# Gated linear attention and four experts on one core: earlier w2 splits, a tile of its own for the last raw w1, and other due times for the attention steps

## The chip, the core and the metric

The kernel runs on one core of a Trainium2 chip. The metric is the device time of one execution in microseconds. Each kernel is run several times and its median is taken; the kernel before has a median of 972.38 us over three runs (972.06 to 972.76). In what follows PE is TensorE (matmuls; PEld its weight loads), ACT is ScalarE, DVE is VectorE, POOL is GpSimd and SP is SyncE, which issues most of the loads.

## The reference

A gated linear attention over 4 batches, 8 heads, 768 tokens and a head width of 48 gives a matrix of 3072 tokens by 384, and four experts with a hidden width of 1024 work on each of its rows, weighted by each token's probabilities.

```python
# attention: q, k, v, alpha of shape (4, 8, 768, 48)
for t in range(S):
    state = alpha[:, :, t, :, None] * state + np.einsum('bhd,bhe->bhde', k[:, :, t], v[:, :, t])
    y[:, :, t] = np.einsum('bhd,bhde->bhe', q[:, :, t], state)
# bridge: (B,H,S,D) -> (B*S, H*D)
x = y.transpose(0, 2, 1, 3).reshape(B * S, H * D)
# experts: w1 (4, 384, 1024), w2 (4, 1024, 384)
p = domain_probs / (domain_probs.sum(-1, keepdims=True) + 1e-09)
for e in range(E):
    h = np.maximum(x @ w1[e], 0.0)
    out += p[:, e:e + 1] * (h @ w2[e])
```

## The kernel before

**Units and groups.** The tokens are cut into 24 units of 128 (six blocks of the sequence, four batches each; the block is the outer loop). Units are counted from 0 here. The attention of a unit (`attention`, for unit 0 `first_unit`) is a generator that does a step and yields: first the transposes of alpha, k and q, with the unit's own terms (`own_terms`, L524), then products of cumulated decays level by level (`next_q` L566, `next_k` L580, the ACT copies at L559 and L579), between them two bursts of small matmuls: the "products" (96 matmuls at L587) and the "far" burst (L663, L668 and L587). DVE takes pieces of their scores into a tile `near` (L597), ACT (L678, L681) and POOL (L686) copy these into `lat`, and then comes the result: matmuls of the state with the queries and of the values with `lat` (`yps`, L708), the copy out of PSUM (L721), the matmuls of the state's update (`sps`, L745) and that update (L753 on DVE in the first block; L755 on POOL and L756 on DVE later).

**Experts.** Units are gathered into seven groups: units 0 and 1, then groups of four, and a last one of two. For each group and expert, `up` multiplies by w1 (eight chunks of the hidden width, index `fc`; result `one`, relu into `hT`) and `down` by w2 (result `ops`, added to `acc` at L926). Group 0 computes in plain fp32 (L820, L905). From group 1 on, weights, inputs and hidden values are held as a rounded top and a remainder, and the product is three matmuls of fp32r parts (L826, L905); the remainder of the hidden values is taken at L851, that of x at L292.

**Weights.** Each expert's w1 and w2 come in four pieces. A raw piece is loaded by `load_piece` (SP, L255). `split_piece` makes its parts: for w2 a POOL cast of the whole (L263), an ACT pass for the top (L268), a DVE subtraction for the remainder (L270), and mostly a store to a kept copy in DRAM (POOL's queue, L276), from which later groups load it (L232, L236, with a short load on POOL's queue, L222). w1 is split while group 0 works, w2 while group 1 does. A split advances by one step with each call of `background`; `making` is the list of splits that have not begun. In the kernel before, the raw w1 of experts 1 to 3 is loaded, in turn, into parts of the tiles that later hold w2 (`shared`), at chunk 4 of the expert before; the raw w2 of the first expert of group 1 is loaded at the end of the last `up` of group 0. Two pieces of it are split in the last `down` of group 0 and two in the first `up` of group 1 (the second entry of `BESIDE`).

**Order.** The order of instructions is written out by hand: each engine does its instructions in the order in which the program issues them. `deal` gives each step of each unit a due time on a clock of estimated costs (`cost`), spread over the time from one group to the next by the shares in `BEATS`; `advance` is called beside every chunk of the experts' work and runs the steps that are due. Two rules in `deal` are touched here: a step waits for the step of the unit before that frees its buffer (`ahead`), and the products of a unit (step 8) are not put closer than 2.5 behind the result (step 16) of the one before. The steps of unit 1 up to its `lat` copies are put by a list of times in the main part; it is worked off, whatever is left of it, after the first `down`.

PSUM has four buffers for `one` and `ops` together, two for scores and two for `yps` and `sps`. SP's and POOL's queues are worked in order too: a load that waits for a buffer or for a store holds back what is issued behind it.

Of the kernel before, what the change touches and what calls it, by code (L numbers as in the profile page):

```python
# [10 lines left out]
F32 = mybir.dt.float32  # L11
F32R = mybir.dt.float32r
# [8 lines left out]
def kernel(  # L21
# [37 lines left out]
    nc = tc.nc  # L59

    B, H, S, D = q.shape
    E, DM, F = moe_w1.shape
    P = 128
# [5 lines left out]
    KC = DM // P  # L69
    FCH = F // P  # L70
    NT = B * P
    NQ = 4
    QF = F // NQ
# [9 lines left out]
    j = np.arange(P)[:, None] % HALF  # L83
# [10 lines left out]
    wts = ctx.enter_context(tc.tile_pool(name="wts", bufs=2))  # L94
# [14 lines left out]
    near = const.tile([P, H, QUAD], F32, name="near")  # L109
# [46 lines left out]
    casts = deque()  # L156
    beat = [0]
    shared = {}
    accs = {}


# [45 lines left out]


    SPLIT_AT = {1: 2, 4: 3}
    BESIDE = [{1: 0, 2: 1, 3: 2, 4: 3}, {1: 2, 2: 3}]  # L210

    def second(rest):
        return wts.tile([P, 1 if rest else 2, KC * QF], F32R, name="w2r" if rest else "w2", bufs=NQ)
# [10 lines left out]
    def load_piece(l, i, beside=False, rest=False):  # L224
        if i >= E * NQ * LAST:
            return
        gi, k = divmod(i, E * NQ)
        e, c = divmod(k, NQ)
        if gi > l and not (l == 1 and fresh(gi, e)):
            if l == 0:  # L230
                w = wt[l][i] = wts.tile([P, 3, KC * QF], F32R, name="w1", bufs=AHEAD)
                nc.sync.dma_start(out=w[:, :2].bitcast(F32), in_=kept[l][k])  # L232
                casts.append((beat[0], lambda: load_short(l, i, w[:, 2])))
                return
            w = second(rest)
            nc.sync.dma_start(out=w[:, :1].bitcast(F32), in_=kept[l][k][:, 1:] if rest else kept[l][k][:, :1])  # L236
            if not rest:
                casts.append((beat[0], lambda: load_short(l, i, w[:, 1])))
            wt[l].setdefault(i, []).append(w)
            return  # L240
        if l == 1 and gi == 0 and not beside:
            return
        if l == 0:

            if e == 0:
                shared[c] = second(True)[:, 0], second(False)[:, 1]
            w = shared[c][e % 2].bitcast(F32)
        elif gi > 0 or e == 1:
            if c == 0:
                shared["w2"] = hid.tile([P, NQ, KC * QF], F32, name="raw2", bufs=1)  # L250
            w = shared["w2"][:, c]
        else:
            w = hidden[c][:, 0].rearrange("p f n -> p (f n)")[:, :KC * QF].bitcast(F32)
        wt[l][i] = w
        nc.sync.dma_start(out=w.rearrange("p (c n) -> p c n", c=(KC, FPQ)[l]), in_=whole_piece(l, i))  # L255

    def split_piece(l, i):
        gi, k = divmod(i, E * NQ)
        whole = wt[l][i]
        if i >= E * NQ:  # L260
            ws = wt[l][i] = [second(False), second(True)]
            top, rest = (w[:, 0] for w in ws)
            nc.gpsimd.tensor_copy(out=ws[0][:, 1], in_=whole)  # L263
        else:
            ws = [wts.tile([P, 3, KC * QF], F32R, name="w1", bufs=AHEAD)]
            top, rest = (ws[0][:, part] for part in range(2))

        nc.scalar.activation(out=top, in_=whole, func=ACT.Copy, scale=LIFT)  # L268
        yield
        nc.vector.tensor_sub(rest, whole, top.bitcast(F32))  # L270
        if (gi, k // NQ) != (1, 0):
            yield
            to = kept[l][k]
            for part, w in enumerate(ws):
                n = 2 - l
                nc.gpsimd.dma_start(out=to[:, part:part + n], in_=w[:, :n].bitcast(F32))  # L276
# [219 lines left out]
    def attention(u):  # L496
# [186 lines left out]
        yield  # L683
        for s in range(P // QUAD):
            rows = slice(QUAD * s, QUAD * (s + 1))
            nc.gpsimd.tensor_copy(out=lat[rows, :, rows], in_=near[rows])  # L686
        KT = KTs[-1]
        yield

# [4 lines left out]
        def result():  # L694
# [16 lines left out]
            if slot == 0:  # L711
# [5 lines left out]
                    xraws[gi] = xraws[gi].rearrange("p (c n) -> p c n", n=NT)  # L717
                else:
                    xraws[gi] = []
            if gi < LAST:  # L720
                nc.scalar.copy(out=xraws[gi][:, :, slot * P:(slot + 1) * P], in_=yps)  # L721
            else:

                xraws[gi].append(AT)
                nc.scalar.copy(out=AT[:, :KC, :], in_=yps)
# [62 lines left out]
    def up(gi, e, fc, slots=None):  # L788
# [13 lines left out]
            making.append(split_piece(1, first_piece(gi, e) + beside[fc]))  # L802
        if gi == 0 and e > 0 and fc in SPLIT_AT:
            making.append(split_piece(0, e * NQ + SPLIT_AT[fc]))
        if gi == 0 and e + 1 < E and fc == FCH // 2 and begins:
            for k in range(NQ):
                load_piece(0, (e + 1) * NQ + k)
            for k in range(NQ if e == 0 else 0):
                load_piece(1, NQ + k, beside=True)
# [24 lines left out]
        background()  # L834
        if f == FPQ - 1 and ends:
            if gi == 0:
                for k in range(NQ if i == E * NQ - 1 else 0):
                    load_piece(1, i + 1 + k)
                for k in range(2 if e == E - 1 and c > 1 else 0):
                    load_piece(0, E * NQ + 2 * (c - 2) + k)  # L840
            elif gi != LAST - 1:
                del wt[0][i]
                load_piece(0, i + AHEAD)
            while late:
                load_piece(1, late.popleft(), rest=True)
            while stores:
                stores.popleft()()
# [6 lines left out]
    def down(gi, e, slots, between):  # L854
# [5 lines left out]
            making.extend(split_piece(0, k) for k in range(NQ))  # L860
        if gi == 0 and e < E - 1 and slots[0] == (e == 0):
            making.extend(split_piece(0, first + NQ + k) for k in range(2))
        if gi == 0 and e == E - 1 and slots[0] == 1:
            making.extend(split_piece(1, first + NQ + k) for k in range(NQ // 2))
        while fresh(gi, e) and (making or splitting):
            background()

# [80 lines left out]
    def deal():  # L948
# [3 lines left out]
        wanted = [0.0]  # L952
        ends = [0.0, 0.0]
        events = []
        times = []
        t = 0.0
        for (gi, e), after in zip(tasks, tasks[1:]):
# [6 lines left out]
        for gis in [*([gi] for gi in range(1, LAST - 1)), [LAST - 1, LAST]]:  # L964
# [9 lines left out]
            for k in range(n):  # L974
                u = sum(map(len, groups[:gi])) + k
                end = due - (n - 1 - k) * space
                begin = max(end - 2 * space, ends[-2])
                ends.append(end)
                run = attention(u)
                times.append([begin + (end - begin) * beat for beat in BEATS])  # L980

                for j in range(1, len(BEATS)):
                    ahead = {4: 12, 7: 14, 13: 16}.get(j)
                    free_at = times[-2][ahead] + 0.5 if ahead and times[:-1] else 0.0
                    if j == 8 and times[:-1] and abs(times[-1][j] - times[-2][16]) < 2.5:
                        free_at = times[-2][16] + 2.5
                    times[-1][j] = max(times[-1][j], times[-1][j - 1] + 0.2, free_at)
                events += [(time, u, run) for time in times[-1]]
        return sorted(events, key=lambda x: x[:2])

    def advance(spent):
# [5 lines left out]
    with tc.manual_schedule():  # L997
# [22 lines left out]
        def fill(times, n=P):  # L1020
            for _ in range(times):
# [5 lines left out]
        nc.sync.dma_start(out=p_all, in_=moe_domain_probs.rearrange("(n p) e -> p n e", p=P))  # L1027

        waiting.extend(sorted([*((at, 1, runs[1]) for at in
                                 (0.4, 1.0, 2.1, 3.1, 4.4, 6.0, 7.2, 8.2, 9.2, 12.4, 12.7, 13.0, 14.9)),  # L1030
                               *((at, 0, runs[0]) for at in (4.0, 12.6))], key=lambda x: x[0]))
        for fc in range(FCH):
            up(0, 0, fc, slice(0, 1))
# [54 lines left out]
```

## Time and profile before

| | us |
|---|---|
| median of three runs | 972.38 |
| lowest and highest | 972.06, 972.76 |
| the profiled execution | 971.66 |
| its span in the profile | 969.9 |
| PE busy | 956.1 |
| DVE busy | 533.8 |
| ACT busy | 419.1 |
| POOL busy | 246.1 |
| mean granted clock of TensorE | 0.997 of full speed |

The busy times are sums over the whole span. Those of PE come from 10252 matmul records, whose ends are modelled, so a busy PE is not one at its peak. The costliest groups of instructions show where PE's time goes; the columns are line, engine, operation, what is written from what, shape and count, then busy time, mean ns of one, and the idle time ahead of it with what ended most of that.

```profile
L826 PE MATMUL one<-xT,w 128*128 128x512 f32 (+1 forms) x1512 | 343.7, 383 | 1.2 <-DVE hT L851 0.7
L905 PE MATMUL ops<-w,hT 128*128 128x384 f32 x1408 | 254.4, 338 | 0.3 <-DVE hT L851 0.3
L905 PE MATMUL ops<-w2r,hT 128*128 128x384 f32 x704 | 127.8, 337 | 0.0
L708 PE MATMUL yps<-lat,rv 128*32 128x128 f32 x736 | 33.6, 273 | 2.7 <-issue 1.4
```

"issue" stands for time in which an engine waited for nothing that the profile shows. Releasers are inferred from semaphore events; where the engine named had long been done, it was another one.

### The profile page before, as it was taken

To read this page: it belongs to the slowest core of one execution; us is meant where nothing else is said; L and a number is where in the kernel's file an instruction comes from. 1 tells how busy PE (TensorE), PEld (TensorE's weight loads), DVE (VectorE), ACT (ScalarE), POOL (GpSimd) and SP (SyncE) were. 2 spreads that over 40 slices of the span, in tenths; PEclk is the share of its full clock that TensorE was granted. 3 is DMA by queue.
4 is the path that set the end of the run, shared out by engine and by line. 5 is a ranking of instruction groups with operands and counts; after the bars stand their busy time and mean duration, and the time that the engine had idled before them with its cause. 6 is when DMAs were issued, how large, how long until landed. Compare 5 with 4: busy or idle time off the path is not lost.

```text
span 969.9 us, 24872 instructions
## 1 busy us (share of the span) xinstructions
PE 956.1 (99%) x10252; PEld 852.9 (88%) x10252; DVE 533.8 (55%) x1126; ACT 419.1 (43%) x973; POOL 246.1 (25%) x403
## 2 busy tenths in 40 slices
PE   8999989999999999999999999999999999999998
PEld 7777769898988989989889899898898999999998
DVE  5666698678678555556546455656665312222312
ACT  4777666456455354433353342555335122121111
POOL 3121142345245322313123123223221202020200
PEclk9999999999999999999999999999999999999999
DMA  9979798998999999999999999999997609192831
GB/s 190 322 239 289 217 345 228 249 378 243 269 335 295 335 322 268 269 328 287 295 325 251 303 262 318 322 255 307 294 309 261 229 1 334 57 314 78 288 102 50
DMA packets 215617, 251.21 MB, mean 259 GB/s; under 512 B 95280, under 2 KB 184752, under 8 KB 215504
## 3 DMA queue, kind: packets, MB, share of 16 engines
q1 hardware_dynamic: 160464, 164.74, 57.7%
q0 software_dynamic: 54592, 84.55, 30.0%
q8 instruction: 81, 1.33, 0.6%
q10 hardware_dynamic: 448, 0.32, 0.1%
q14 instruction: 32, 0.26, 0.1%
HBM read 219.69 MB, written 29.88 MB: 257 GB/s over the span
## 4 chain that ended last, share of the span: by engine, by line
PE 95%; DMA 2%; DVE 1%; issue 1%; ACT 0%; POOL 0%; SPq 0%; DVEq 0%; ACTq 0%; POOLq 0%
PE ops L905 42%; PE one L826 37%; PE one L820 4%; PE yps L708 4%; PE sc L587 3%; PE tp L307 2%; DMA sa<-in_alpha_dram 1%; PE sc L663 1%; PE sps L745 1%; DMA sk<-in_k_dram 1%; PE sc L668 1%; PE sc L367 0%; POOL lat L686 0%; PE idle L1022 0%; PE y L478 0%
## 5 line engine op out<-in xcount | busy, mean ns | idle before, releaser
L826 PE MATMUL one<-xT,w 128*128 128x512 f32 (+1 forms) x1512 | 343.7, 383 | 1.2 <-DVE hT L851 0.7
L826 PEld LDWEIGHTS one<-xT,w 128*128 128x128 f32 x1512 | 271.6, 188 | 54.4 <-DVE hT L851 1.3
L905 PE MATMUL ops<-w,hT 128*128 128x384 f32 x1408 | 254.4, 338 | 0.3 <-DVE hT L851 0.3
L905 PEld LDWEIGHTS ops<-w,hT 128*128 128x128 f32 x1408 | 243.2, 188 | 3.0 <-DVE hT L851 0.5
L828 ACT ACTIVATE hT<-one 128x512 fp32r<-128x512 f32 (+1 forms) x200 | 109.1, 547 | 282.4 <-PE one L826 281.4
L851 DVE SCALAR_TENSOR_TENSOR hT<-one,hT 128x512 fp32r<-128x512 f32 (+1 forms) x200 | 125.1, 628 | 172.4 <-ACT hT L828 172.1
L222 POOL DMA_DIRECT2D w<-in_moe_w_dram x140 | 106.0, 758 | 390.9 <-PE one L826 282.7
L905 PE MATMUL ops<-w2r,hT 128*128 128x384 f32 x704 | 127.8, 337 | 0.0
L905 PEld LDWEIGHTS ops<-w2r,hT 128*128 128x128 f32 x704 | 122.1, 188 | 0.3 <-issue 0.2
L559 ACT COPY qb<-QT 64x256 f32<-64x256 f32 x230 | 92.4, 402 | 28.6 <-DVE QT L566 26.9
L566 DVE TENSOR_TENSOR QT<-QT,AT 128x256 f32<-128x256 f32 x158 | 71.8, 455 | 34.7 <-ACT qb L559 29.8
L926 DVE SCALAR_TENSOR_TENSOR acc<-ops,p_all,acc 128x384 f32<-128x384 f32 x66 | 39.6, 612 | 84.8 <-PE ops L905 84.7
L580 DVE TENSOR_TENSOR KT<-KT,AT 128x256 f32<-128x256 f32 x161 | 74.9, 465 | 0.0
L597 DVE COPY_PREDICATED near<-masks,sc 128x128 f32<-128x128 uint8 x115 | 40.9, 356 | 60.7 <-PE sc L587 58.9
L686 POOL COPY lat<-near 32x256 f32<-32x256 f32 x92 | 44.4, 482 | 75.4 <-DVE near L597 72.1
L550 ACT ACTIVATE odd<-QT,ident 64x256 f32<-64x256 f32 x36 | 18.9, 524 | 68.1 <-DVE QT L508 67.8
L579 ACT COPY KT<-KT 128x256 f32<-128x256 f32 x115 | 47.1, 409 | 2.5 <-DVE KT L580 0.3
L568 DVE TENSOR_TENSOR AT<-AT 128x256 f32<-128x256 f32 (+1 forms) x138 | 43.1, 312 | 4.7
L755 POOL TENSOR_TENSOR st<-st,dec 64x192 f32<-64x192 f32 x32 | 16.6, 520 | 95.4 <-PE yps L708 94.2
L550 ACT ACTIVATE odd<-QT 64x256 f32<-64x256 f32 x46 | 20.1, 436 | 47.8 <-DVE QT L566 47.5
L708 PE MATMUL yps<-lat,rv 128*32 128x128 f32 x736 | 33.6, 273 | 2.7 <-issue 1.4
L826 PE MATMUL one<-KT,w 128*128 128x256 f32 x288 | 34.6, 279 | 0.0
(133 smaller groups left out, 899.5 us busy)
## 6 DMA issues: line engine op xcount, KB each, us to landing
w<-kept SPq DMA_DIRECT2D x80, 768.0 KB, 7.1
w<-in_moe_w_dram POOLq DMA_DIRECT2D x140, 384.0 KB, 8.6
w<-kept SPq DMA_DIRECT2D x60, 384.0 KB, 6.7
w2r<-kept SPq DMA_DIRECT2D x60, 384.0 KB, 7.4
kept<-w POOLq DMA_DIRECT2D x16, 768.0 KB, 6.1
raw<-in_moe_w_dram SPq DMA_DIRECT2D x24, 384.0 KB, 10.3
kept<-w POOLq DMA_DIRECT2D x16, 384.0 KB, 8.3
kept<-w2r POOLq DMA_DIRECT2D x16, 384.0 KB, 8.4
```

What stands on the lines that cost most here:

```text
L222: nc.gpsimd.dma_start(out=out.rearrange("p (c n) -> p c n", c=(KC, FPQ)[l]), in_=whole_piece(l, i))
L559: nc.scalar.copy(out=qb[rows, :, i, :].rearrange("p a (b r) -> p a b r", r=m), in_=qv[rows])
L566: nc.vector.tensor_mul(qv, qv, spread(dv[:, :, :, 0], m))
L568: nc.vector.tensor_mul(dec, dv[:, :, :, 0], dv[:, :, :, 1])
L579: nc.scalar.copy(out=new[:, :, :, 1, :], in_=old[:, :, :, 1, :])
L580: nc.vector.tensor_mul(new[:, :, :, 0, :], old[:, :, :, 0, :], spread(halved(decs[li])[:, :, :, 1], m))
L686: nc.gpsimd.tensor_copy(out=lat[rows, :, rows], in_=near[rows])
L708: nc.tensor.matmul(yps[QUAD * j:QUAD * (j + 1), c, :], lhsT=lhsT, rhs=rhs, start=begins, stop=ends)
L826: nc.tensor.matmul(one, lhsT=w[:, (0, 2, 1)[part], kc], rhs=x_part(gi, part % 2, kc)[:, lo:hi], start=(part == 1 and kc == 0), stop=(part ...
L828: nc.scalar.activation(out=parts[0], in_=one, func=ACT.Relu)
L851: nc.vector.scalar_tensor_tensor(out=low, in0=x, scalar=0.0, in1=top.bitcast(F32), op0=ALU.max, op1=ALU.subtract)
L905: nc.tensor.matmul(sums[slot], lhsT=h, rhs=w, start=(n == begins[slot]), stop=(n == ends[slot]))
```

## The change

Five edits, all in the order of work and in where pieces lie; what is computed stays the same, and so does the number of matmuls.

1. The raw w2 of the first expert of group 1 is loaded one expert sooner, at the end of the up stage of expert 2 of group 0. Its first two pieces are split in the `down` of that expert, the other two at chunks 3 and 6 of the last `up` of group 0. Nothing of it is left for the first `up` of group 1.
2. The raw w1 of expert 3 goes into the third part of the w1 tile that its split will use (`last_w1`), two pieces after each of the last two quarters of the up stage of expert 2.
3. Units 2 to 5 (those of group 1) have other shares for their last five steps: 0.66, 0.68, 0.72, 0.78 and 0.79 where the others have 0.69, 0.745, 0.85, 1.0 and 1.01 (and 0.64 ahead of them as before), and the unit behind them begins from their new end.
4. Where the products of a unit fall within 2.5 of the result of the unit before, that result is drawn ahead (but stays 4.0 behind its step before), and the products come at least 5.0 behind it.
5. For unit 1, the second and fourth of the last `lat` copies go to DVE, the copy of its result is made in three parts (ACT, DVE, ACT), and its last listed step is due at 14.4.

```diff
-    BESIDE = [{1: 0, 2: 1, 3: 2, 4: 3}, {1: 2, 2: 3}]
+    BESIDE = [{1: 0, 2: 1, 3: 2, 4: 3}, {}]
...
+            if e == E - 1:
+                last_w1[c] = wts.tile([P, 3, KC * QF], F32R, name="w1", bufs=AHEAD)
+            w = (last_w1[c][:, 2] if e == E - 1 else shared[c][e % 2]).bitcast(F32)
...
-            ws = [wts.tile([P, 3, KC * QF], F32R, name="w1", bufs=AHEAD)]
+            ws = [last_w1[k % NQ] if k // NQ == E - 1 else wts.tile([P, 3, KC * QF], F32R, name="w1", bufs=AHEAD)]
...
-            nc.gpsimd.tensor_copy(out=lat[rows, :, rows], in_=near[rows])
+            (nc.vector if u == 1 and s % 2 else nc.gpsimd).tensor_copy(out=lat[rows, :, rows], in_=near[rows])
...
-            if gi < LAST:
+            if u == 1:
+                for c, copy in enumerate((nc.scalar.copy, nc.vector.tensor_copy, nc.scalar.copy)):
+                    copy(out=xraws[gi][:, c, slot * P:(slot + 1) * P], in_=yps[:, c])
+            elif gi < LAST:
...
+        if gi == 0 and e == E - 1 and fc in (3, 6):
+            making.append(split_piece(1, E * NQ + 1 + fc // 3))
         if gi == 0 and e + 1 < E and fc == FCH // 2 and begins:
-            for k in range(NQ):
+            for k in range(NQ if e + 1 < E - 1 else 0):
                 load_piece(0, (e + 1) * NQ + k)
...
-                for k in range(NQ if i == E * NQ - 1 else 0):
-                    load_piece(1, i + 1 + k)
+                for k in range(2 if e == E - 2 and c > 1 else 0):
+                    load_piece(0, (E - 1) * NQ + 2 * (c - 2) + k)
+                for k in range(NQ if e == E - 2 and c == NQ - 1 else 0):
+                    load_piece(1, E * NQ + k)
...
-        if gi == 0 and e == E - 1 and slots[0] == 1:
-            making.extend(split_piece(1, first + NQ + k) for k in range(NQ // 2))
+        if gi == 0 and e == E - 2 and slots[0] == 1:
+            making.extend(split_piece(1, E * NQ + k) for k in range(NQ // 2))
...
-                times.append([begin + (end - begin) * beat for beat in BEATS])
+                beats = BEATS if gi > 1 else BEATS[:13] + [0.66, 0.68, 0.72, 0.78, 0.79]
+                times.append([begin + (end - begin) * beat for beat in beats])
+                ends[-1] = times[-1][-1]
...
-                    if j == 8 and times[:-1] and abs(times[-1][j] - times[-2][16]) < 2.5:
-                        free_at = times[-2][16] + 2.5
+                    if j == 8 and times[:-1]:
+                        before, at = times[-2], times[-1][j]
+                        if abs(at - before[16]) < 2.5:
+                            before[16] = min(before[16], max(before[15] + 4.0, at - 5.0))
+                            free_at = before[16] + 5.0
...
-                events += [(time, u, run) for time in times[-1]]
+                runs_at.append((u, run))
+        for (u, run), at in zip(runs_at, times):
+            events += [(time, u, run) for time in at]
...
-                                 (0.4, 1.0, 2.1, 3.1, 4.4, 6.0, 7.2, 8.2, 9.2, 12.4, 12.7, 13.0, 14.9)),
+                                 (0.4, 1.0, 2.1, 3.1, 4.4, 6.0, 7.2, 8.2, 9.2, 12.4, 12.7, 13.0, 14.4)),
```

## The prediction, written before the changed kernel was run

> **What bounds the kernel now.** I read the shares by engine first (TensorE busy 956.1 of the 969.9 us span), then the windows of 20 us, to see where the other 13.8 us are, then TensorE's waits, and last the timelines around each wait. In the windows the columns are the busy time of PE, PEld, DVE, ACT and POOL with the number of instructions, the granted clock, the share of the DMA engines and GB/s.
>
> ```profile
> 120.00:140.00 20.00, 18.56 (x250) 13.20 (x245) 18.18 (x35) 11.90 (x32) 11.12 (x16) 1.00 1.12 384
> 140.00:160.00 20.00, 18.46 (x341) 17.08 (x341) 18.72 (x44) 13.17 (x33) 2.16 (x5) 1.00 0.91 211
> 160.00:180.00 20.00, 19.30 (x275) 18.62 (x274) 11.49 (x28) 12.08 (x32) 8.70 (x13) 1.00 1.07 314
> 180.00:200.00 20.00, 19.80 (x174) 16.88 (x174) 16.71 (x31) 12.62 (x26) 7.22 (x12) 1.00 0.80 221
> 200.00:220.00 20.00, 20.00 (x336) 18.76 (x335) 13.69 (x31) 8.45 (x20) 7.18 (x13) 1.00 1.11 362
> ```
>
> TensorE is full from 40 to 120 us and again from 200 us on, so a change of order there can gain nothing unless it removes matmuls, and this one removes none. What can be won lies between 120 and 200 us: 1.44 + 1.54 + 0.70 + 0.20 = 3.9 us. The waits (total us, times, longest) name them:
>
> ```profile
> PE yps L708 <- issue: 1.4, 1, 1.4
> PE yps L708 <- POOL lat L686: 1.2, 1, 1.2
> PE sc L587 <- issue: 0.9, 1, 0.9
> PE one L826 <- DVE hT L851: 0.7, 1, 0.7
> PE one L820 <- ACT xT L721: 0.6, 1, 0.6
> PE one L826 <- DVE acc L926: 0.5, 1, 0.5
> PE ops L905 <- DVE hT L851: 0.3, 1, 0.3
> ```
>
> Two of them wait for nothing that the profile shows. In the timeline (start, length, work, count, idle before it) they stand in the middle of bursts of small matmuls:
>
> ```profile
> 123.76 0.39 PE L708 MATMUL yps<-lat,rv 128*32 128x128 f32 x5
> 125.59 0.30 PE L708 MATMUL yps<-lat,rv 128*32 128x128 f32 x2 [1.44 <-issue]
> 178.74 0.55 PE L587 MATMUL sc<-qb,KT 128*32 128x32 f32 x38
> 180.20 0.41 PE L587 MATMUL sc<-qb,KT 128*32 128x32 f32 x26 [0.90 <-issue]
> ```
>
> The queue table shows what they are:
>
> ```profile
> q8 instruction: 81, 1.33, 0.6%
> ```
>
> 81 packets in 1.33 MB is 16 KB each, and TensorE's list of some 20,700 instructions (matmuls, weight loads, semaphores) divided by 81 is 256. Counted in that list, these two stops and the one "issue" wait at the start fall at positions 449, 3521 and 5057, which are apart by multiples of 256, and the instruction packet began 2.4 to 2.6 us before TensorE went on (123.00 to 125.59 us; 177.84 to 180.20). So TensorE here ran through a block of 256 instructions faster than the next one came. Both blocks hold two bursts: the products of unit 5 (119.11) close ahead of the result of unit 4 (122.43), and the result of unit 6 (173.64) close ahead of the products of unit 7 (178.27). Without the stop they would have taken about 4.2 us; blocks of 5.7 us and more did not stop. [...]
>
> The other three waits come from VectorE running late at the first expert of the second group. VectorE and GpSimd from 135 us:
>
> ```profile
> 135.23 2.85 POOL L263 CAST w<-raw 128x768 fp32r<-128x768 f32 x3
> ...
> 135.48 0.93 DVE L568 TENSOR_TENSOR AT<-AT 128x256 f32<-128x256 f32 x1
> 136.33 1.05 DVE L580 TENSOR_TENSOR KT<-KT,AT 128x256 f32<-128x256 f32 x1
> 139.97 0.41 DVE L566 TENSOR_TENSOR QT<-QT,AT 128x256 f32<-128x256 f32 x1
> 141.49 1.81 DVE L270 TENSOR_TENSOR w2r<-raw,w 128x768 fp32r<-128x768 f32 x2
> ```
>
> While GpSimd casts, a 128x256 operation of VectorE takes 1.05 us instead of 0.41; then four w2 remainders (L270) of 0.9 to 0.96 us stand between the hT remainders that the matmuls wait for.
>
> **The change, part by part.** The sum goes against the profiled execution, 971.66 us (1.8 of it around the span); the median of the runs is 972.38, 0.72 more, which I add at the end.
>
> *Results sooner, bursts apart.* Matmuls, copies and weight loads are the same in number; only their places in the queues move. In the new order of TensorE I cut the list at the same residue of 256 and priced each block from the rows (0.216 us for a w1 matmul of 256 columns, 0.34 for one of 384, 0.65 + 0.79 for the products, 2.8 for a result without its stop). The shortest blocks come to 4.95, 5.53, 5.64 and 5.8 us; none holds the old pairs. Bounds: all of 1.44 + 0.90 = 2.34 goes, or, if the one of 4.95 stops as 4.2 did, 0.8 of it returns. I take the whole, -2.34, because that block begins and ends in large matmuls, like the blocks that ran through.
>
> *First w2 splits sooner.* Each of four pieces is a ScalarE pass (0.85), a GpSimd cast (0.96) and a VectorE remainder (0.95). They leave the stretch of 135 to 148 us: VectorE loses 3.7 us of remainders there and some 2.7 us of slowed operations (five of them, about 0.55 each). What is left for it is about 11.4 us of work over 10 us of TensorE work, with four PSUM buffers between them as slack. I count the three waits as gone: -(0.46 + 0.73 + 0.34) = -1.53; bounds 0 and -1.53.
>
> The same pieces arrive an expert sooner, in the last expert of the first group, and there they are paid. VectorE's list for that up stage rises from 9.2 to 16.3 us of work (two or three w2 remainders, a w1 remainder, unit 5's levels, and the first steps of unit 6, which the earlier due times pull in: three transposes of 1.1 each and the 0.55 + 0.55 own terms). TensorE works there for some 14 us: 48 x 0.216, the result of unit 4 with its state update (2.8), products (1.2). What comes late next is unit 5's far burst, which waits for its level 16 and 8 keys: VectorE reaches them only behind unit 6's own terms. From 107.0 us (end of a w1 remainder before) the list up to the own terms adds to 15.5 us, so 122.5 to 123.0; from there two own terms 1.1, two level steps 2.0, two takes 0.93, a transpose 1.1, a w2 remainder 0.95 and a ScalarE copy 0.5 make 6.5: 129.0 to 129.5. TensorE would be there at 130.34 - 1.44 = 128.9. That is the lower end, 0.1 to 0.6.
>
> The upper end is set by the loads. SyncE's queue in order: two loads of the last raw w1 now wait for stores of earlier pieces (a store issued at 92.07 takes 6.1), so the four raw w2 loads go out at about 98.5 to 101; they land 7.0 to 10.3 later. The sooner cast on GpSimd waits for the first, and behind it in that queue is the small memset that releases unit 6's key load; behind that on SyncE are its other key load, four raw w2 loads for expert 3, the query loads and the last one, rq:
>
> ```profile
> 106.08 0.15 POOL L188 MEMSET sk<- 128x64 f32 x1 [1.05 <-DVE rk L526]
> ...
> 115.94 0.41 SPq L198 DMA_DIRECT2D rq<-in_q_dram x1
> ```
>
> With the first piece landed at 106.5 the memset slips by 1.4 to 2.4, and so would rq: issued at 117.3 to 118.3, landed 6.4 to 7.2 later, 123.7 to 125.5. VectorE's own term of unit 6 waits for rq and everything behind it on VectorE too, so the far burst would come at up to 132.0 to 132.5: 3.6. I take +1.2, nearer the lower end, because SyncE issued its four sk loads in 4.52 us where four sq loads took 1.95, so the queue has some room to catch up. If the cover of the early w2 landing is gone altogether, the price is that of the slower rival.
>
> *The w1 tile for the last raw w1* frees the w2 tiles for the splits and moves no work but these loads: costed with them.
>
> *Tail of the second unit.* GpSimd's two last copies go to VectorE, and the one result copy becomes three on two engines. But TensorE waited for both engines here:
>
> ```profile
> 36.10 1.07 ACT L681 COPY lat<-sc 32x128 f32<-32x128 f32 x4
> ...
> 35.46 1.73 POOL L686 COPY lat<-near 32x256 f32<-32x256 f32 x4 [13.21 <-DVE near L597]
> ```
>
> ScalarE ends at 37.17 and GpSimd at 37.19, so a faster GpSimd is worth 0.02. VectorE has its state copies until 36.78 and would end its two at 37.3 to 37.6. The three result copies are chained by their waits (VectorE's behind ScalarE's first, ScalarE's second behind VectorE's): the first third is there some 0.2 sooner, the last no sooner than the 0.48 us copy was. Bounds -0.3 and +0.4; I take +0.2.
>
> **Sum:** -2.34 - 1.53 + 1.2 + 0.2 = -2.47: 969.19 for the profiled execution, 969.9 with the 0.72.
>
> **Rivals.** *Everything clean:* the far burst finds VectorE in time and the tail costs nothing: -3.9, 968.5. For it: VectorE has idle stretches of 3.67 us before 115.44 that early work could fill. *The stall only moves:* the far burst of unit 5 waits 2.5 us and the tail takes 0.4: 971.66 - 3.87 + 2.9 + 0.72 = 971.4, no change. For it, the 16.3 us of VectorE work over 14 of TensorE; against it, the 0.3 to 1.3 us by which units 2 and 3 have their parts ready. *The fetches stay:* blocks stop elsewhere, or the stops are something else: the 2.34 comes back, 972.2; if half of it, 971.1. [...] *Slower:* the raw w2 loads, held behind the last w1 store, land 10.3 us after issue, as the median of the other raw w2 loads does (108.8); cast and memset end near 110.0, the key loads take their 4.5 us again, and with 0.5 + 2.4 + 2.0 for what follows rq leaves at 119.5 to 120 and lands at 126.5 to 127. Then the own term is 4 us late, the far burst comes near 133.3, 4.4 late, and unit 5's result and the next group's xT remainders behind it another 1.5: 971.66 - 3.87 + 5.9 + 0.2 + 0.72 = 974.6. It decides from rq landing after about 126.5. For it: the store and the cast are single links without spare buffers; against it, the DMA share of 0.82 between 100 and 120 us.
>
> **How the numbers follow.** About 0.2%, 1.9 us, is what a measurement here can tell from no change. Forecast 0.43, clean 0.08, stall moved 0.18, fetches stay 0.15, slower 0.16. The first two are faster (0.51), the next two within (0.33), the last slower (0.16). The likeliest case alone spans 968.4 to 970.6. The range reaches from the clean case less 1 us for uncounted pace around the stops, 967.4, up through the moved stall and the stayed fetches to just short of the slower case, 974.0.
>
> **What would show it.** After the change the two issue waits in the result of unit 4 and the products of unit 7 are gone and no other of over 0.8 us has come; hT and acc waits of TensorE between 140 and 150 us are gone; L270 on w2r is at 112 to 128 us; a wait of 0.5 to 2 us stands ahead of unit 5's far burst (L663 before) near 129 us; the wait for lat near 37 us is between 1.2 and 1.7. The windows from 200 us on are as full as before. The prediction is wrong if issue waits reappear with the sum of 2 us, if the far burst waits over 3 us, or if any window after 200 us shows TensorE idle.

## The result and the profile after

The changed kernel takes 978.58 us (978.36 to 979.14, four runs) beside 972.29 for the kernel before: a ratio of 1.0065 (95% interval 1.0048 to 1.0082), 6.3 us slower. Its profiled execution has a span of 977.3 us against 969.9.

TensorE's waits in the changed kernel (total us, times, longest; line numbers have moved by 3 to 10: L666 was L663, L751 was L745, L711 was L708, L735 was L729):

```profile
PE sc L666 <- ACT qb L562: 4.5, 1, 4.5
PE sps L751 <- ACT AT L735: 3.1, 1, 3.1
PE yps L711 <- DVE lat L689: 1.6, 1, 1.6
PE y L481 <- issue: 1.4, 1, 1.4
```

All five waits between 120 and 200 us that the prediction counted as gains are gone, the two stops for "issue" and the three for VectorE. Two new and longer ones stand in their place: unit 5's far burst, and the state update of unit 5's result. Behind 200 us TensorE is as full as before. At the start a stop for "issue" of 1.4 us came (L481, at 20.8 us), longer than the 0.8 that the prediction allowed; a second profile of the same kernel (changed_again) does not have it. The windows (busy PE, PEld, DVE, ACT, POOL; granted clock, DMA share, GB/s):

```profile
120.00:140.00 20.00, 15.48 (x204) 10.85 (x203) 17.17 (x36) 9.76 (x25) 7.66 (x12) 0.91 1.17 340
140.00:160.00 20.00, 16.80 (x263) 13.86 (x262) 11.65 (x27) 10.14 (x28) 1.51 (x2) 0.91 0.57 106
160.00:180.00 20.00, 19.89 (x281) 19.03 (x280) 15.15 (x42) 14.04 (x37) 6.63 (x10) 1.00 0.89 257
180.00:200.00 20.00, 20.00 (x241) 18.07 (x241) 10.71 (x23) 8.60 (x20) 4.86 (x8) 1.00 0.72 209
```

TensorE idles 7.8 us in these 80, against 3.9 before, and 1.0 more in the first 40. That is 4.9 of the 7.4 us by which the span grew. The other 2.6 are in the busy time, 958.7 us instead of 956.1 for the same number of records, 10252: work got slower. It is a net figure, for the kernel before has a low clock at its start (0.91 from 0 to 20 us) that this execution has not (1.00). The granted clock (seventh figure) shows when, in windows of 4 us:

```profile
128.00:132.00 4.00, 1.28 (x4) 0.40 (x3) 3.87 (x10) 2.15 (x5) 1.06 (x2) 1.00 1.10 331
132.00:136.00 4.00, 2.20 (x65) 2.07 (x66) 1.78 (x7) 1.74 (x6) 0.00 (x0) 0.69 1.45 303
136.00:140.00 4.00, 4.00 (x14) 2.42 (x14) 3.66 (x8) 0.57 (x2) 3.42 (x6) 0.88 1.12 365
140.00:144.00 4.00, 3.59 (x61) 2.14 (x59) 2.27 (x7) 3.78 (x12) 0.58 (x1) 1.00 1.21 227
144.00:148.00 4.00, 1.20 (x33) 0.92 (x34) 2.25 (x7) 2.82 (x7) 0.93 (x2) 0.90 0.78 110
148.00:152.00 4.00, 4.00 (x19) 2.98 (x18) 0.86 (x3) 0.38 (x1) 0.00 (x0) 0.68 0.25 49
```

After each of the two waits the clock is low in one or two of these windows. In narrower ones it is 0.50 from 133.6 to 136.9 and from 147.2 to 150.5 us, and 1.00 around. TensorE's timeline (start, length, work, count, idle ahead) gives the price:

```profile
124.60 4.68 PE L915 MATMUL ops<-hT 128*128 128x384 f32 x14
133.80 1.08 PE L666 MATMUL sc<-qb,KT 128*32 128x128 f32 x16 [4.52 <-ACT qb L562]
...
135.67 3.46 PE L915 MATMUL ops<-hT 128*128 128x384 f32 x8
138.97 0.60 PE L310 MATMUL tp<-ident,KT 128*128 128x128 f32 x4
...
146.80 0.58 PE L751 MATMUL sps<-rv,AT 128*32 128x48 f32 x32 [3.07 <-ACT AT L735]
147.31 2.93 PE L915 MATMUL ops<-hT 128*128 128x384 f32 x4
```

In the kernel before:

```profile
126.27 4.14 PE L905 MATMUL ops<-hT 128*128 128x384 f32 x12
130.34 0.64 PE L663 MATMUL sc<-qb,KT 128*32 128x128 f32 x16
```

The first 16 matmuls of the far burst take 1.08 us where they took 0.64. The four fp32 matmuls at 147.31 hold TensorE for 2.15 us, up to the next group's start at 149.46 (the 2.93 has a modelled end), 0.54 each; the twelve before held it for 4.07, 0.34 each. Now the engines that TensorE waits for. VectorE and ScalarE:

```profile
116.04 0.96 DVE L273 TENSOR_TENSOR w<-w 128x768 fp32r<-128x768 f32 x1 [1.46 <-ACT w L271]
...
119.37 0.35 DVE L762 TENSOR_TENSOR st<-st,sps 64x192 f32<-64x192 f32 x1 [1.18 <-POOL st L761]
...
126.00 1.28 DVE L529 TENSOR_TENSOR rk<-rq,rk 128x384 f32<-128x384 f32 x1
...
131.84 0.42 DVE L583 TENSOR_TENSOR KT<-KT,AT 128x256 f32<-128x256 f32 x1
```

```profile
132.02 1.02 ACT L789 ACTIVATE xT<-x_raw 128x256 fp32r<-128x256 f32 x3
132.95 0.80 ACT L562 COPY qb<-QT 64x256 f32<-64x256 f32 x2
...
146.16 0.58 ACT L735 COPY AT<-tp 128x512 f32<-128x512 f32 x1
```

VectorE comes to unit 6's own terms (L529) at 126.0, having waited 1.46 and 1.18 us on the way, and to unit 5's level behind them at 131.8; ScalarE then does the tops of x (L789) before the two copies that the far burst needs. At 146.16 the turned keys of unit 5 are copied (L735: the transposed keys that the state update multiplies), whose transposes TensorE had done at 139.6 (L310 above); nine copies for unit 6, issued ahead of it between 142.20 and 146.16, had to go first. The last load of unit 6 was not late:

```profile
116.56 0.39 SPq L199 DMA_DIRECT2D rq<-in_q_dram  x1
```

It landed 6.0 us later, at 122.6, and VectorE came to it at 126.0.

### The profile page after: what moved, and what is told of

It is laid out like the page before. It is cut to its first block, busy times and chain, and to the rows that moved or that the text cites. A ratio compares the mean times of both kernels' runs of the same rounds, so it can differ in the third digit from the quotient of the medians.

```text
span 977.3 us, 24884 instructions
## 1 busy us (share of the span) xinstructions
PE 958.7 (98%) x10252; PEld 853.8 (87%) x10252; DVE 532.7 (55%) x1129; ACT 419.9 (43%) x974; POOL 245.5 (25%) x401
## 4 chain that ended last, share of the span: by engine, by line
PE 93%; DVE 2%; ACT 2%; DMA 1%; issue 1%; SPq 0%; POOL 0%; DVEq 0%; POOLq 0%
PE ops L915 41%; PE one L834 37%; PE one L828 3%; PE yps L711 3%; PE sc L590 3%; PE tp L310 2%; PE sc L666 1%; DMA sq<-in_q_dram 1%; PE sps L751 1%; PE sc L671 1%; DMA sa<-in_alpha_dram 0%; DVE QT L569 0%; ACT qb L562 0%; PE idle L1040 0%; ACT odd L553 0%
## 5 line engine op out<-in xcount | busy, mean ns | idle before, releaser
L761 POOL TENSOR_TENSOR st<-st,dec 64x192 f32<-64x192 f32 x32 | 16.9, 527 | 102.7 <-PE yps L711 101.5
L915 PE MATMUL ops<-hT 128*128 128x384 f32 x96 | 35.7, 515 | 0.0
L711 PE MATMUL yps<-lat,rv 128*32 128x128 f32 x736 | 33.4, 273 | 1.8 <-DVE lat L689 1.6
```

The source lines that it names most:

```text
L711: nc.tensor.matmul(yps[QUAD * j:QUAD * (j + 1), c, :], lhsT=lhsT, rhs=rhs, start=begins, stop=ends)
L915: nc.tensor.matmul(sums[slot], lhsT=h, rhs=w, start=(n == begins[slot]), stop=(n == ends[slot]))
```

## The experiments

"Before" ran beside each group of kernels, on the same chip. All ratios are to it; u6 is unit 6.

| kernel | median us | before | ratio (95% interval) |
|---|---|---|---|
| u6_late | 969.44 | 973.05 | 0.9965 (0.9952 to 0.9978) |
| splits_back | 977.38 | 973.05 | 1.0045 (1.0030 to 1.0060) |
| only_splits | 974.23 | 973.05 | 1.0013 (1.0000 to 1.0026) |
| tail_back | 977.47 | 973.05 | 1.0054 (1.0036 to 1.0073) |
| u6_levels_late | 976.07 | 972.83 | 1.0043 (1.0025 to 1.0061) |
| u6_first_late | 977.42 | 972.83 | 1.0057 (1.0041 to 1.0074) |
| warm | 981.04 | 972.83 | 1.0097 (1.0080 to 1.0113) |
| u6_late_tail | 969.01 | 972.83 | 0.9967 (0.9956 to 0.9979) |
| u6_behind | 972.75 | 972.56 | 0.9998 (0.9989 to 1.0007) |
| late_no_splits | 967.95 | 972.56 | 0.9951 (0.9939 to 0.9964) |
| warm18 | 979.83 | 972.56 | 1.0078 (1.0063 to 1.0093) |
| shift | 981.26 | 972.56 | one run |
| changed_again | 979.62 | 972.56 | 1.0062 (1.0039 to 1.0086) |
| warm_even | 980.70 | 972.56 | 1.0075 (1.0055 to 1.0096) |
| only_apart | 971.71 | 972.56 | 0.9985 (0.9973 to 0.9997) |
| results_only | 970.09 | 972.56 | 0.9969 (0.9957 to 0.9982) |

### Which edit makes it slow

**u6_late**: one line less.

```diff
-                ends[-1] = times[-1][-1]
```

> The changed kernel with one line taken out: the unit behind unit 5 does not begin from unit 5's new end, so unit 6's first nine steps are due where they were in the kernel before (its first one at 65.5 instead of 59.0 on the due-time clock); unit 2 to 5 keep their sooner results, the splits their new place. Theory A (the steps of unit 6, drawn ahead of unit 5's last levels and ahead of its turned-keys copy on VectorE and ScalarE, hold TensorE): the 4.5 us wait ahead of unit 5's far burst falls to under 1 us, the 3.1 us wait of the state update's matmuls for the turned keys to under 0.5, the granted clock stays at 1.00 between 120 and 160 us, and the time falls from 978.6 to 969 to 972. Theory B (the w2 splits put into that stage are what makes VectorE late): the far burst still waits 3 us or more and the time is 975 or more.

TensorE's timeline in u6_late:

```profile
131.95 0.65 PE L666 MATMUL sc<-qb,KT 128*32 128x128 f32 x16
...
137.35 0.63 PE L310 MATMUL tp<-ident,KT 128*128 128x128 f32 x4 [1.46 <-DVE KT L583]
```

Theory A as expected: the far burst waits for nothing, the state update neither, the clock is 1.00, and the time goes from 6.3 us above the kernel before to 3.4 below it (1.0065 and 0.9965). One line makes more than 9 us. What is left is 1.5 us of unit 5's keys waiting for VectorE. By the rules of `deal` the line draws unit 7 ahead as well (its first step by 5.8 on the due-time clock) and puts later units back by at most 0.6; the two runs that move unit 6 alone, below, tell which of its steps made the waits.

**splits_back**: edits 1 and 2 undone, the line kept.

> The changed kernel with the w2 splits and the last raw w1 put back to where they were before (edits 1 and 2 undone), the due times as changed. Theory A: of the two long waits only what two w2 remainders (0.95 each) and the slowed operations beside the casts cost goes away, 2 to 2.5 us of the 4.5 at the far burst, nothing of the 3.1 at the turned keys, and the waits of 0.3 to 0.7 us for VectorE at the first expert of the second group come back: 976 to 979. Theory B: both long waits go: 970 to 973.

Its waits:

```profile
PE sps L748 <- ACT AT L732: 3.0, 1, 3.0
PE sc L663 <- ACT qb L559: 2.3, 1, 2.3
```

Theory A again: half of the first wait was the splits' share, none of the second, and it stays slower than before. The small waits for VectorE at the first expert of the second group, expected back, did not come.

**only_splits**: edits 1 and 2 alone.

> The kernel before with edits 1 and 2 alone (w2 splits an expert sooner, the last raw w1 in its own tile); due times and tail as before. Theory A: the three waits of 0.46, 0.73 and 0.34 us for VectorE at 140 to 150 us go, the far burst of unit 5 waits under 1 us, the two issue waits (1.4 and 0.9) stay: 970 to 972.5. Theory B: a wait of 2 us or more at unit 5's far burst: 974 or more.

Between the theories, and a miss. Unit 5's far burst does not wait, but others do:

```profile
PE one L831 <- DVE acc L933: 2.4, 1, 2.4
...
PE sc L590 <- ACT qb L562: 1.6, 1, 1.6
PE sc L590 <- issue: 1.5, 1, 1.5
```

The wait for `acc`, 0.46 before, is 2.4, and unit 5's products, in the stage that the splits went to, wait 1.6 for a copy for which VectorE was late. The last line is the stop in unit 7's products; the one at unit 4's result, expected to stay, is gone too, though its burst was not moved. Alone, the edit that takes work from VectorE at 140 us gains nothing.

**tail_back**: edit 5 undone.

> The changed kernel with the tail of the second unit as before (edit 5 undone). If the shared tail costs what the trace of the changed kernel suggests (the wait for the last lat copies 1.6 instead of 1.2 us, that for the result copy 0.4 instead of 0.6): the wait is again for GpSimd's copies at 1.2, and the time falls by 0.2 to 0.4, to about 978.3; both long waits stay.

```profile
PE yps L711 <- POOL lat L689: 1.2, 1, 1.2
...
PE one L825 <- ACT xT L724: 0.6, 1, 0.6
```

The two waits are as expected (1.2 and 0.6 for 1.6 and 0.4, so 0.2). In the time, 1.0054 and 1.0065 overlap, and u6_late (0.9965) beside u6_late_tail (0.9967) shows nothing either: too small to settle by times.

### Which order makes which wait

**u6_levels_late** and **u6_first_late** take the early steps of unit 6 apart; TensorE's order is that of the changed kernel in both.

```diff
-                    ahead = {4: 12, 7: 14, 13: 16}.get(j)
+                    ahead = {4: 15 if u == 6 else 12, 7: 14, 13: 16}.get(j)
```

> The changed kernel with one number changed: unit 6's step 4 and those behind it are due only after unit 5's turned-keys copy (71.8 instead of 69.2 on the due-time clock); its first steps stay early. TensorE's order is the same, 13 places on ScalarE and 8 on VectorE change: the turned-keys copy of unit 5 now stands ahead of nine copies of unit 6. If the second long wait is ScalarE's order (the copy queued behind unit 6's copies, which each wait for VectorE): the 3.1 us wait for the turned keys falls to under 0.5, the first wait stays between 4.0 and 4.6, and the time falls by 3 to 4.5, to 974 to 975.5. If it only follows from the first wait (everything is late): it stays at 2 us or more and the time moves by less than 1.

```profile
133.28 1.08 PE L666 MATMUL sc<-qb,KT 128*32 128x128 f32 x16 [4.54 <-ACT qb L562]
...
143.77 0.52 PE L751 MATMUL sps<-rv,AT 128*32 128x48 f32 x32
```

The second wait is gone and the first is untouched, so the second is ScalarE's order and no echo of the first. The time falls by 0.0022, some 2 us (the intervals overlap), less than expected. In the profiled run the clock was 0.53 and 0.62 in the windows from 132 to 140 us, lower than in the changed kernel; whether that is the rest is not shown.

```diff
                 ends[-1] = times[-1][-1]
+                if u == 6:
+                    times[-1][:4] = [65.5, 66.8, 67.9, 69.0]
```

> The reverse: unit 6's first four steps are due where u6_late had them (65.5 to 69.0), step 4 and those behind it stay early (69.2). TensorE's order is the same; on VectorE the two transposes, unit 6's own terms and the query transpose now stand behind unit 5's last levels. If the first long wait is VectorE's order: the wait ahead of unit 5's far burst falls from 4.5 to under 0.7, the wait for the turned keys stays between 1.5 and 3.5, and the time falls by 4 to 6, to 972.5 to 974.5. If the splits are what makes it late, the far burst still waits 2.5 or more.

```profile
129.22 0.64 PE L666 MATMUL sc<-qb,KT 128*32 128x128 f32 x16
...
134.46 0.63 PE L310 MATMUL tp<-ident,KT 128*128 128x128 f32 x4 [1.30 <-DVE KT L583]
...
144.19 0.87 PE L751 MATMUL sps<-rv,AT 128*32 128x48 f32 x32 [2.29 <-ACT AT L735]
```

The first wait is gone, so it was VectorE's order; but the time falls by 0.8 us at most, within the noise, not 4 to 6. TensorE is early at the next things and waits there: 1.3 for the keys, 1.9 in the result (put down to "issue"; the instruction is not at an end of a block of 256. What it waited for stays open; until 139.42, beside its start at 139.23, ScalarE was writing pieces of `lat`, which it reads), 2.3 for the turned keys, and the clock is 0.50 from 140 to 148 us. Only both orders together (u6_late) bring the time back.

### What the clock costs

**warm**: 36 needless matmuls in the wait.

```diff
+        for _ in range(36 if u == 5 else 0):
+            nc.tensor.matmul(bank[:, :P], lhsT=ident, rhs=ident, start=True, stop=True)
```

> The changed kernel with 36 needless matmuls of the identity (128x128, overwritten at once) ahead of unit 5's far burst, about 4 us of work inside the wait of 4.5. If the granted clock falls because TensorE stood idle (0.69 from 132 to 136 us, 0.88 to 140): it stays at 0.95 or more there, the far burst takes 1.1 to 1.2 us instead of 1.9, the 8 fp32 matmuls behind it 2.8 instead of 3.5, and the time falls by 1 to 1.6. If the clock has another cause: the same 0.69, and the time is the same or longer. The wait for the turned keys stays in either case.

The clock stayed at 1.00 and the far burst took 0.65 for its first 16, but the filling, two records for each matmul, took 8.2 us in a wait of 4.5, and the kernel is slower. **warm18** has 18, **warm_even** 64 that make 256 records:

```diff
+        for m in [P] * 12 + [QUAD] * 52 if u == 5 else []:
+            nc.tensor.matmul(bank[:m, :m], lhsT=ident[:, :m], rhs=ident[:, :m], start=True, stop=True)
```

> As warm, with 18 needless matmuls in place of 36: the 36 took 8.2 us, so 18 take 4.1 and end before unit 5's far burst is released (4.5). If the fall of the granted clock after the wait costs time by itself: the clock stays at 0.95 or more from 132 to 140 us, the far burst takes 1.1 instead of 1.9 us, and the ratio to the kernel before is 1.0045 to 1.0055, against 1.0065 of the changed kernel (1 to 2 us). If the lower clock is only shown and costs nothing: 1.0065.

> The changed kernel once more, unaltered, so that the next one is compared with it on the same chip: 1.0065 of the kernel before, with the two long waits (4.5 and 3.1) and the low granted clock behind them.

> The changed kernel with 64 needless matmuls ahead of unit 5's far burst (12 of 128x128 and 52 of 32 columns; by the rows 12 x 0.23 and 52 x 0.025, 4.0 us inside the wait of 4.5), 256 records, so that every later block of 256 is cut where it was. If the lower clock costs time: the far burst takes 1.1 instead of 1.9 us, the clock stays near 1.00 from 132 to 140 us, and the time is 1 to 2 us under changed_again. If it costs nothing, the same within 0.5; if the extra instructions bring a stop of their own, an issue wait shows it and the time is longer.

TensorE in warm18:

```profile
127.35 4.68 PE L917 MATMUL ops<-hT 128*128 128x384 f32 x14
131.87 4.18 PE L664 MATMUL sc<-ident 128*128 128x128 f32 x36
136.61 0.64 PE L668 MATMUL sc<-qb,KT 128*32 128x128 f32 x16 [0.56 <-ACT qb L562]
...
140.82 2.10 PE L917 MATMUL ops<-hT 128*128 128x384 f32 x6
```

From the start of the 14 matmuls to the end of the 6 it takes 15.6 us; in the changed kernel 16.9 (124.60 to 141.5). The far burst is released at the same point of it in both (9.3 and 9.2 us behind the start), so the low clock costs 1.3 us at this wait. The whole time did not fall, though. warm18 shifted TensorE's later blocks and got a new stop of 1.1 us at 694 us; warm_even's filling took 6.2 us and ran some 1.3 us past the release (135.88, where 9.2 us behind the 14 matmuls would be 134.5), which used up the gain on the spot, and the clock after the second wait was 0.50 instead of 0.68. The local price is shown; that it can be won back is not.

### Which part gains

**u6_late_tail** is u6_late with edit 5 undone; **late_no_splits** undoes edits 1 and 2 as well; **only_apart** is edit 4 alone and **results_only** edit 3 alone (without the line).

> The changed kernel without its one line that draws unit 6 ahead (as in u6_late) and with the tail of the second unit as before. If the two parts are separate: the wait of u6_late for the last lat copies goes from 1.6 back to 1.2, and the ratio to the kernel before is that of u6_late (0.9965) less 0.0002 to 0.0005. The late VectorE transposes still hold the turned keys' matmuls by 1.5.

> u6_late_tail with edits 1 and 2 undone: only the sooner results and the bursts apart are left of the change. By the prediction's terms: the two issue waits (1.4 and 0.9) are gone, the three waits of 0.46, 0.73 and 0.34 for VectorE at 140 to 150 us are back, the late transposes do not hold the turned keys by more than 0.5 because the w2 remainders are elsewhere: 0.9970 to 0.9980. If the splits' new place is worth nothing: as u6_late_tail, 0.9967 or lower.

> The kernel before with edit 4 alone (bursts at least 5.0 apart where they were within 2.5; it moves the results of units 6, 9 and 17). If the gain of a stop that goes is kept: the 0.9 us stop in unit 7's products goes, the 1.4 at unit 4's result and the three waits for VectorE stay: a ratio of 0.9987 to 0.9995.

> The kernel before with the sooner results of units 2 to 5 alone (edit 3 without the line that draws unit 6 ahead; no splits moved, bursts as before). If the parts add up: late_no_splits (0.9951) less only_apart, so 0.9955 to 0.9965; the 1.4 us stop at unit 4's result gone, the 0.9 one in unit 7's products there. If the three waits for VectorE come from the splits at that place alone, they stay at 1.5 together or grow by the 1.4 that TensorE now comes sooner; if unit 5's result in that stage was part of what made VectorE late, they shrink to under 1.

late_no_splits has the lowest median of the study, 4.6 us under the kernel before. Its windows, and its waits between 60 and 200 us:

```profile
120.00:140.00 20.00, 20.00 (x310) 14.19 (x309) 18.27 (x39) 14.29 (x36) 9.21 (x15) 1.00 1.12 353
140.00:160.00 20.00, 19.09 (x273) 18.16 (x273) 19.61 (x43) 12.70 (x32) 3.65 (x7) 1.00 1.00 257
```

```profile
PE one L826 <- DVE hT L851: 0.7, 1, 0.7
PE one L826 <- DVE acc L926: 0.2, 1, 0.2
```

The parts add up: 0.9969 for the sooner results and 0.9985 for the bursts apart multiply to 0.9954. The waits behind VectorE came down from 1.5 to 0.9 us without moving a split. With the splits moved (u6_late_tail) the ratio is 0.9967: by the medians their new place costs about 1.5 us here and 1.3 alone (1.0013), but the intervals of the two kernels overlap and that of the second reaches 1.0000. In the traces between 60 and 200 us TensorE waits 1.7 us with the splits moved and 0.9 without. In only_apart the stop in unit 7's products is gone while that at unit 4's result was 2.3 us in this profile; in results_only it is the other way round, with 1.0 us left in unit 7's products.

**u6_behind**: unit 6's first step due behind unit 5's far burst, against the 1.5 us that u6_late_tail still waits.

```diff
+                if u == 6:
+                    times[-1][0] = max(times[-1][0], times[-2][12] + 0.2)
```

> u6_late_tail with unit 6's first step due no sooner than unit 5's far burst (68.9 instead of 65.5), so that on VectorE its three transposes and own terms (some 4.4 us) stand behind unit 5's last key level. TensorE's order is the same. If the 1.5 us wait of unit 5's turned keys for VectorE in u6_late_tail is these transposes: it falls to under 0.3, and the ratio to the kernel before goes from 0.9967 to 0.9950 to 0.9957 (1 to 1.5 us). If a remainder of x behind them (one of the three now stands after the transposes) becomes late for the first expert of the next group: a wait of 0.5 to 1.5 at its first matmuls and a ratio of 0.996 to 0.998.

```profile
PE sps L748 <- ACT AT L732: 3.2, 1, 3.2
```

A miss that teaches: the 1.5 us are gone, but ScalarE's order now has copies of unit 6 that wait for the late transposes ahead of unit 5's turned keys, and the gain is lost.

### What the "issue" stops are

**shift**: the kernel before with half a block more on TensorE's list at the start.

```diff
         fill(7)
+        fill(32, 8)
```

> The kernel before with 32 needless fp32 matmuls of 8 columns at its very start, 128 matmul and weight-load records (64 and 64): half a block of 256. Nothing else moves. If the issue waits are blocks of 256 instructions that TensorE ran through faster than the next came: both waits at unit 4's result and unit 7's products (1.4 and 0.9) are gone, and from the times of the blocks as they would then be cut in the trace of before, new ones of 0.7 to 1.5 us come in the state update of unit 3's result (about 101 us, a block of 4.7 us) and in products near 587 us (4.5 us); all at the same remainder of 256 as before. If they belong to the work itself (the close bursts), they stay where they were. The time rises by up to 4 us from the start.

Both stops (1.4 and 0.9 us in the kernel before) are gone though the bursts stand as close as before, so they belong to the blocks and not to the work. In all traces every stop for "issue" of 0.3 us or more is at 193 of 256 in TensorE's list (449, 705, 3521, 5057, in warm18 16577; one place further where the weight load of the pair is counted first), but for the one of 1.9 us in u6_first_late. The new ones did not come: the blocks of 4.69 and 4.49 us (as they would be cut in the trace of before, up to 101.28 and 586.86 us) ran through, their packets having begun 4.1 and 3.4 us ahead. Counted alike, from one cut to the next, the blocks that stopped at 125.59 and 180.20 us in the kernel before took 4.62 and 4.53 us without their stops, where the prediction has about 4.2. So a block's time does not tell the two kinds apart; what starts the packet stays open. The time cannot be compared: the fillers held up the start by over 10 us (the first expert's matmuls begin at 32.0 us instead of 21.3), not by the 4 expected. But the wait behind is telling:

```profile
PE one L826 <- DVE acc L926: 1.8, 1, 1.8
```

With the 1.4 us stop gone, TensorE comes sooner to the wait for `acc`, which grows from 0.46 to 1.8: that gain is given back 16 us later, unless VectorE gains as well.

## Why the prediction was wrong

The forecast was 969.9 us, in a range up to 974.0; the result is 978.58. Between the profiled executions the span grew by 7.4 us: -3.9 for the five waits that went, 4.5 and 3.1 for the two that came, 0.2 for small ones, 1.0 at the start and 2.6 of slower work make 7.5.

- *Results sooner, bursts apart, -2.34.* The mechanism was right: both stops are gone and none came behind them, though that the shortest blocks run through was a choice between two bounds. By the medians edits 3 (without its line) and 4 give more, 4.6 us (3.5 to 5.9 by the interval). The two profiled executions differ by 2.9, which the stops (2.3) and shorter waits for VectorE (0.6) make up; where the rest comes from stays open.
- *First w2 splits sooner, -1.53.* The three waits are gone as said, but as an edit it gains nothing: by the medians it costs about 1.3 us alone and 1.5 beside the others, at the edge of what the runs can tell. The relief at 140 us came with the sooner results too.
- *What comes late next, +1.2.* This is the step that failed. "From 107.0 us (end of a w1 remainder before) the list up to the own terms adds to 15.5 us, so 122.5 to 123.0" summed VectorE's durations and left out its own waits: VectorE began at 107.55 and stood still for 3.3 us (1.46 for a split's ScalarE pass, 1.41 for the state on GpSimd behind a cast, 0.47 for scores), and reached the own terms at 126.0. The 6.5 us behind them were 7.8: ScalarE began the two copies only at 132.95, for its tops of x and copies of unit 6 stood in that queue. The far burst came at 133.8 instead of 129.0 to 129.5; even the upper end, 132.5, was too low, and the wait of 4.5 us is over the 3 that the prediction named as a sign of being wrong. The cause is shown by u6_first_late and u6_late, where unit 6's first steps stand behind unit 5's levels and the wait is gone, and by splits_back, where 2.3 us of it are left.
- The upper end was hung on the loads. rq left at 116.56, sooner than the 117.3 to 118.3 feared; the loads held nothing. The rival on the slower side named the right place and nearly the right time (133.3) with the wrong cause.
- *Not in the sum at all:* the wait for unit 5's turned keys, 3.1. The steps of unit 6 that are drawn ahead were followed on VectorE and on the queues of loads, not on ScalarE, where nine copies stand ahead of one that TensorE needs.
- *Not in the sum either:* the clock, which was 0.50 for 3.41 us behind each of the two waits (133.53 to 136.94 and 147.18 to 150.60 us). Behind the first wait, of 4.5 us, the mean from 132 to 136 us is 0.69, and behind the second, of 3.1 us, it is 0.68 from 148 to 152, while splits_back's 3.0 left the clock at 1.00. So a stall cost more than itself here: there were 7.6 us of waits, and behind the first 1.3 of slower work.
- *Tail, +0.2.* By the waits 1.6 + 0.4 against 1.2 + 0.6, it is that; the times can't show it.

## What to carry to other kernels

A step that is drawn ahead must be followed on every engine that it issues to, and the question at each is which instruction, needed sooner by the bottleneck, now stands behind it. A due time for a queue is worked out with that queue's own waits, not from a sum of durations. And an edit made of parts is worth taking apart: here, by the medians, the sooner results and the bursts apart gained 4.6 us, the splits' new place cost some 1.5 (not clear of the noise), and one line more than 9.

## What the runs showed of the hardware

Behind TensorE's waits of 4.5 and 3.1 us in the changed kernel the granted clock was 0.50 for 3.41 us each, and the wait of 4.5 cost 1.3 us beyond itself (16.9 us from the 14 matmuls to the end of the 6, against 15.6 in warm18). The length of a wait alone does not decide. A stop of 2.3 us in only_apart left the clock at 1.00 from 120 to 160 us, where in u6_first_late it was 0.50 from 140 to 148 behind a wait of 1.9 that ended at 139.23 (the wait of 2.3, from 141.9 to 144.19, lies inside that stretch). In splits_back the clock was low behind the wait of 2.3 us (0.69 from 132 to 136), and not behind that of 3.0, which ended at 144.95:

```profile
140.00:144.00 4.00, 1.96 (x57) 1.47 (x56) 2.83 (x5) 3.16 (x9) 2.85 (x4) 1.00 1.17 382
144.00:148.00 4.00, 3.05 (x46) 2.45 (x47) 2.85 (x6) 2.83 (x5) 1.72 (x3) 1.00 1.05 359
```

In the traces of the kernel before and of the changed kernel the granted clock is 1.00 or 0.50, and the times between its changes are 3.41, 10.24, 126.29, 826.02 and 948.90 us: 1, 3, 37, 242 and 278 times 3.413. In such steps, counted back from its low stretches, the changed kernel's waits of 4.5 and 3.1 us fill 3.4 and 3.0 us of the step just ahead (130.12 to 133.53 and 143.77 to 147.18 us), while splits_back's wait of 3.0 us, counted on from its low stretch, falls into two steps, 1.8 and 1.2 us. Whether this is what decides is not shown: no run moves a wait against the steps.

At the start TensorE was slow without a wait: in shift, 78 records of needless matmuls (64 of them 8 columns wide) took 16.8 us, 0.215 each, where in warm 72 took 8.2, 0.114 each, and four transposes took 1.06 to 1.09 us up to 21 us and 0.66 from 22.6 on. The granted clock reads 1.00 in that stretch, so the profile does not show why.

The kernel before has 20,730 instructions in TensorE's list and 81 instruction packets of 16 KB, 256 to a packet, and its three stops for "issue" (1.4, 1.4 and 0.9 us) stand at positions that are multiples of 256 apart. With 128 records more at the start (shift) none of the three came, and the filling of warm18 at 131.87 us was followed by a stop of 1.1 us at 694, over 500 us behind the edit and again at 193 of 256.
